# Stationary operand as neighbouring columns, stores in 128-byte pieces and another opening order in a one-core attention and MoE kernel

## The chip, the cores and the metric

The kernel runs on one core of a Trainium2 chip. The metric is the device time of one execution, in microseconds (us). The kernel before takes 589.66 us, the median of three runs (589.54 to 589.89).

## The reference, cut to what matters

```python
# attention with a decaying state, B=2, H=8, S=768, D=64
for t in range(S):
    state = gamma * state + outer(k[t], v[t])
    y[t] = scale * q[t] @ state
x = y.transpose(0, 2, 1, 3).reshape(1536, 512)
# first expert layer, 512 -> 1536 -> 512
x = x / sqrt(mean(x * x) + 1e-6) * rms_g
x = (silu(x @ w_gate) * (x @ w_val)) @ w_out
# second layer, 512 -> 2048 -> 512
h = x @ w_in
out = maximum(0.01 * h, h) @ w_out2
```

All inputs and the output are float32 (the kernel reads the weights as 64-bit numbers and makes two float32r parts of each: a high part and the rest).

## The kernel before, in words

The 1536 tokens are 12 chunks of 128 for the attention and three blocks of 512 (b = 0, 1, 2) for the two layers. The feature dimension of the weights is cut into rows or columns f of 128.

**The opening** is written out by hand, token by token, in `ORDER` (lines 42 to 56). Each engine runs the tokens that concern it in the order of this list, and none overtakes another on its engine. `load("q0")`, `load("k0")` and so on, in the order of `LOADS` (line 33), bring in what a chunk needs; a `w` in `LOADS` brings the next raw weight into one of three raw buffers (`fetch`, line 379). All these transfers are issued by SyncE into one queue. The tokens of a chunk c, with the engine in brackets: `sc` scores (TensorE), `ds` decay of the scores (VectorE), `kd` decay of k (VectorE if c is in `KD`, else eight activations on ScalarE), `qs` decay of q (GpSimd), `ou` outer product and `up` state update (TensorE, VectorE), `yi` and `he` the two parts of the chunk's output y (TensorE), `sq` square of y and `xg` y times the gain (ScalarE, both read y from PSUM), `fa` and `sa` the first two sums of the squares (VectorE). `to`, `me`, `rs`, `sp`, `xs`, `hi`, `lo` form the norm of a pair of chunks and split it into high part and rest. y has two PSUM banks, for even and odd chunks (line 226), so `yi8` may not start before `sq6` and `xg6` have read y of chunk 6.

Weights are converted in steps such as `o0:P`, `o0:1`, ... `o0:L`, for the weight o of f = 0. `:P` is two activations on ScalarE that read the raw buffer (lines 526 and 527), `:1` to `:4` are VectorE steps, `:H` the high part on ScalarE, `:L` the rest on VectorE. Step `:3` is the last that reads the raw buffer, and it calls `fetch` for the next raw weight. The raw weights come in the order g0, g1, v0, v1, o0, o1: the three `w` of `LOADS` bring the first three, `g0:3` fetches v1, and the next `:3` in the list fetches o0. The token `load` brings q11 and k11; it stands ahead of every `:3`, so v1 and o0 follow k11 in the queue.

The token `layers` marks the end of the attention on TensorE; `Mg00`, the first product of the first layer (the high parts), comes right behind it.

**The layers** run from a list of steps made by `plan`. Three kinds of product matter here, each a group of matmuls of 128x128 against 128x512:
- line 587 (`accumulate`), the down products. For the first layer (`o`) and for the blocks b > 0 of the second (`p`), the weight is the stationary operand, 128 of its columns at a time. For `p` with b = 0 the activations are stationary.
- line 706 (`seventh`), the down products of the last two groups of `p`, by sums of weights, also with the weight stationary.
- lines 554 and 858, the up products.

For `p` the 128 stationary columns are chosen by `by_quarter`: every second column of one half of 256. Two neighbouring output columns thus end up in one partition of two accumulators (m = 0 and 1). For `o` they are 128 neighbouring columns.

**The end.** When the last sums of a row of blocks are complete, `seventh` transposes the two accumulators in 32x32 blocks, with m as the innermost dimension (line 729), and stores the result in four transfers of 128 KB whose contiguous pieces are 64 floats, 256 bytes (lines 732 to 737). There are four such rows: (b, row) = (2, 0), (2, 1), (1, 0), (1, 1). Block 0 is stored last, from line 751.

Of the kernel before, what the change touches and what calls it, by code (L numbers as in the profile page):

```python
# [8 lines left out]
F32 = mybir.dt.float32  # L9
# [7 lines left out]
P = 128  # L17
# [12 lines left out]
SEVEN = 2  # L30
RAWS = 3
WARM = 7
LOADS = "q0 k0 m g s k1 q1 d q2 q3 k2 k3 q4 k4 q5 w w q6 w q7 k6 k8 k7 k5 i q8 q9 k9 q10 k10"
EARLY = 5
FIXED = 14
PLAIN = ("g0", "g1", "v0", "v1")
# [1 line left out]
BLOCKS = [512, 512, 512]  # L38


KD = (0, 1, 2, 3, 6, 7)
ORDER = """
sc0 kd0 ou0 ds0 tb ts wm1 tk he0 load kd1 up0 sc1 sq0 qs1 xg0 ou1 ds1 qs2 sc2 up1 fa0 yi1 qs3 ds2 he1 kd2 sa0 ou2 kd3
sq1 sc3 xg1 fa1 up2 qs4 yi2 ds3 kd4 ou3 sa1 sc4 up3 qs5 sc5 ds4 g0:P yi3 ds5 ou4 g1:P g0:1 he2 up4 g0:2 he3 g1:1 sq2
g0:3 to0 xg2 fa2 g1:2 sc6 me0 sa2 sq3 rs0 g0:4 sc7 xg3 ds6 v0:P yi4 kd6 ds7 ou6 qs7 kd8 he4 up6 yi5 kd7 v0:1 sq4 fa3
ou7 g0:H fa4 he5 sa3 xg4 g0:L up7 sq5 v0:2 sc8 sa4 xg5 fa5 v0:3 sc9 qs9 ds8 yi7 kd9 ds9 qs8 ou8 sp0 v0:4 to1 up8 qs10
he7 v0:H xs0 kd10 he6 me1 sa5 rs1 g1:3 sc10 v0:L sq6 g1:4 sq7 ou9 fa6 xg6 sc11 up9 fa7 xg7 sa7 yi8 ds11 g1:H yi9 hi0
qs11 ds10 ou10 o0:P he8 lo0 to2 up10 sq8 he9 sa6 me2 g1:L xg8 rs2 to3 fa8 sp1 o0:1 sq9 me3 yi10 xs1 rs3 xg9 fa9 hi1
yi11 sa8 sa9 o0:2 v1:P lo1 sp2 he10 v1:1 he11 xs2 sq10 xg10 layers Mg00 v1:2 fa10 v1:3 hi2 sa10 v1:4 Ng00 sq11 lo2
o1:P Mg10 fa11 xg11 o1:1 o0:3 Ng10 v1:H sa11 o1:2 Cg00 v1:L sp3 Cg10 o1:3 to4 xs3 Mv00 me4 o1:4 hi3 rs4 o0:4 Nv00 lo3  # L50
o0:H Mv10 g2:P o0:L Cv00 o1:H g2:1 Uo00 sp4 o1:L to5 g3:P xs4 Nv10 Mg01 me5 Lo00 hi4 rs5 Cv10 lo4 Uo10 sp5 Ng01 Lo10
xs5 Mg11 Cg01 g3:1 hi5 g2:2 g3:2 Ng11 g2:3 open lo5 Do00 Cg11 g2:4 g3:3 g2:H T0 v2:P Mg02 g3:4 T1 g3:H Ng02 v3:P g3:L
Do10 v2:1 Cg02 v3:1 Th1 v2:2 v3:2 v2:3 Tl1 Mg12 v2:4 v3:3 v2:H Ng12 g2:L v3:4 Mv01 sg2:1 Cg12 v2:L v3:H sg2:2 v3:L
sg2:H Nv01 sg2:3 sg2:L Mv11 sv2:1 Cv01 sv2:2 sg2:4 Nv11 sv2:H sv2:3 T2 sg2:h Mv02 Cv11 Th2 sg2:l Nv02 Tl2 o3:P Mv12
sv2:4 o2:P T3 Nv12 Cv02 Cv12
"""


# [1 line left out]
def chain_kernel(ctx: ExitStack, tc: tile.TileContext, qk_t, kv, w1, w2, mask, qdec, kdec, sdec, rms_g, ident, out):  # L60
    nc = tc.nc
# [8 lines left out]
    offs = [sum(BLOCKS[:b]) for b in range(NB)]  # L70
    assert sum(G1) == NF1 and sum(G2) == NF2

    units = ctx.enter_context(tc.tile_pool(name="units", bufs=UNITS))
# [30 lines left out]
    def acc_bank(i, name):  # L104
        return ps_acc.tile([P, 512], F32, tag=f"acc{i}", name=name)
# [41 lines left out]
    def decay_k(c):  # L147
        if not last(c):
            s = ch[c]
            s["kd"] = gp.tile([P, 2 * NPAIR, D], F32, tag="gh", name=f"kd{c}")  # L150
            if c in KD:
                nc.vector.tensor_tensor(
# [221 lines left out]
    def free(*keys):  # L374
        for s in slots:
            s[2].difference_update(keys)
# [181 lines left out]
    def acc_banks(name, n):  # L558
        return [acc_bank(i, f"{name}_{i}") for i in range(n)]
# [7 lines left out]
    parts = {}  # L567
    order = []

    def by_quarter(w, m):  # L570
        return w.rearrange("p (h c m) -> p h m c", h=2, m=2)[:, m // 2, m % 2]

    def accumulate(L, g, f, b, start, stop, transposed):

        if start:
            acc["b"] = acc_banks(f"a{L}_{g}_{b}", 4)
        h, l = parted.pop((L, f, b))
        w = wt[f"{L}{f}"]
        for m in range(4):
            part = slice(m * P, (m + 1) * P)  # L580
            if transposed:
                wh, wl = (w[:, i, part] if L == "o" else by_quarter(w[:, i, :], m) for i in range(2))
                terms = (wh, h), (wh, l), (wl, h)
            else:
                terms = (h[:, part], w[:, 0, :]), (h[:, part], w[:, 1, :]), (l[:, part], w[:, 0, :])
            for n, (lhs, rhs) in enumerate(terms):
                nc.tensor.matmul(out=acc["b"][m], lhsT=lhs, rhs=rhs, start=(start and n == 0), stop=(stop and n == 2))  # L587
# [3 lines left out]
    def upper(key):  # L591
        if key in made:
            x = made.pop(key)
            h = gp.tile([P, 512], F32R, tag="gh", name="g{}_{}_{}h".format(*key))
            nc.scalar.activation(out=h, in_=x, func=AF.Copy)
            halves[key] = x, h

    def lower(key):
        if key in halves:
            x, h = halves.pop(key)  # L600
            l = gp.tile([P, 512], F32R, tag="gl", name="g{}_{}_{}l".format(*key))
            nc.vector.tensor_tensor(out=l, in0=x, in1=h.bitcast(F32), op=ALU.subtract)
            parted[key] = h, l
            if key[0] == "q":
                follow(key[1], key[2])
# [9 lines left out]
    def down(gi, f, b):  # L615
        kinds, fs = groups[gi]
        L = kinds[-1]
        key = (L, f, b)
        upper(key)
        lower(key)  # L620
        accumulate(L, gi, f, b, f == fs[0], f == fs[-1], L == "o" or b > 0)
        used(f"{L}{f}")
        if f == fs[-1]:
            (evac1 if L == "o" else evac2)(gi, b, acc.pop("b"))
        placed[0] = order.index(key) + 1
# [37 lines left out]
    def gather(gi):  # L663
        for f in groups[gi][1][::2]:
            t = {(k, b): made.pop(("p", f + k, b)) for k in range(2) for b in (1, 2)}
            made["q", f, 1], made["q", f, 3], made["q", f, 2] = t[0, 1], t[1, 2], t[1, 1]
            turns[f] = t
# [22 lines left out]
    def seventh(gi, n, f):  # L690
        fs = groups[gi][1]
        key = ("q", f, n)
        if n == 1 and f == fs[0]:
            gather(gi)
        upper(key)
        lower(key)
        h, l = parted.pop(key)
        unit, half, side, start, (b, row) = SIDES[n]
        names = f"p{f}", f"p{f + 1}", f"sp{f}", f"sp{f + 1}"
        w = wt[names[unit]]  # L700
        if f == fs[0] and start:
            acc[side] = [acc_bank(i + 2 * (side == "Z"), f"{side}{gi}_{n}_{i}") for i in range(2)]
        for m in range(2):
            wh, wl = (by_quarter(w[:, i, :], 2 * half + m) for i in range(2))
            for k, (lhs, rhs) in enumerate(((wh, h), (wh, l), (wl, h))):
                nc.tensor.matmul(  # L706
                    out=acc[side][m],
                    lhsT=lhs,
                    rhs=rhs,
                    start=(start and f == fs[0] and k == 0),  # L710
                    stop=(f == fs[-2] and k == 2),
                    skip_group_check=True,
                )
        if n == 1:
            used(names[0])
        elif n == 4:
            used(names[1])
        elif n in (7, 3):
            free(names[unit])
        placed[0] = order.index(key) + 1  # L720
        if f != fs[-2]:
            return
        for m in range(2):
            dst = y2[b][:, 2 * row + m, :]
            nc.vector.tensor_tensor(out=dst, in0=acc[side][m], in1=dst, op=ALU.add)
        if gi == len(groups) - 1 and LAST[b, row] == n:
            t = units.tile([P, 16, 32, 2], F32, tag="u", name=f"turned{b}_{row}")
            for m in range(2):
                nc.vector.transpose(
                    out=t[:, :, :, m], in_=y2[b][:, 2 * row + m, :].rearrange("p (j r) -> p j r", r=32)  # L730
                )
            for i in range(4):
                o = 2 * row * P + i * 64
                nc.sync.dma_start(
                    out=out[offs[b]:offs[b] + 512, o:o + 64].rearrange("(j r) d -> r j d", r=32),
                    in_=t[32 * i:32 * i + 32].rearrange("p j c m -> p j (c m)"),
                )

    def evac2(gi, b, banks):
        first, last = gi == len(G1), gi == len(groups) - 1  # L740
# [12 lines left out]
    y2 = {}  # L753
# [70 lines left out]
    def used(key):  # L824

        n, f = key[0], int(key[1:])
        left[key] = left.get(key, 2 if doubled(n, f) else NB) - 1
        if not left[key]:
            free(key)
# [190 lines left out]
    nc.scalar.dma_start(out=kdecs[:, 0], in_=kdec)  # L1020
    load(*LOADS.split())

# [28 lines left out]
    terms = {}  # L1051
# [142 lines left out]
```

## Time and profile before

| | us |
|---|---|
| median of three runs | 589.66 |
| the profiled execution | 589.67 |
| its span, first to last instruction | 587.9 |
| TensorE matmul busy | 579.5 |
| VectorE busy | 480.8 |
| ScalarE busy | 343.5 |
| GpSimd busy | 19.5 |

All times below are counted from the start of the span. Busy time is a union of the instructions' times; a matmul's end is modelled, and it overlaps the next one, so the distance between the starts of matmuls (their pitch) says more than the duration of one. PE is the matmul stream of TensorE, PEld its weight loads, DVE VectorE, ACT ScalarE, SPq the queue of SyncE's transfers.

### The profile page before, as it was taken

To read this page: it belongs to the slowest core of one execution; us is meant where nothing else is said; L and a number is where in the kernel's file an instruction comes from. 1 tells how busy PE (TensorE), PEld (TensorE's weight loads), DVE (VectorE), ACT (ScalarE), POOL (GpSimd) and SP (SyncE) were. 2 spreads that over 40 slices of the span, in tenths; PEclk is the share of its full clock that TensorE was granted. 3 is DMA by queue.
4 is the path that set the end of the run, shared out by engine and by line. 5 is a ranking of instruction groups with operands and counts; after the bars stand their busy time and mean duration, and the time that the engine had idled before them with its cause. 6 is when DMAs were issued, how large, how long until landed. Compare 5 with 4: busy or idle time off the path is not lost.

```text
span 587.9 us, 8302 instructions
## 1 busy us (share of the span) xinstructions
PE 579.5 (99%) x3131; PEld 478.4 (81%) x3131; DVE 480.8 (82%) x865; ACT 343.5 (58%) x624; POOL 19.5 (3%) x20
## 2 busy tenths in 40 slices
PE   8899999999999999999999999999999999999997
PEld 6788788888888888888888888888888888888885
DVE  5899999999668689598589988874776679997893
ACT  2789656778655455465564766776563665574430
POOL 2332100000000000000000000000000000000000
PEclk9999999999999999999999999999999999999999
DMA  8991240524133013124130310422211110110043
GB/s 336 408 386 42 72 144 3 175 74 146 39 96 102 18 67 108 36 72 126 54 107 2 103 41 0 144 71 73 72 37 36 37 36 6 67 37 0 1 101 114
DMA packets 23319, 52.76 MB, mean 90 GB/s; under 512 B 10480, under 2 KB 10608, under 8 KB 23280
## 3 DMA queue, kind: packets, MB, share of 16 engines
q1 hardware_dynamic: 23136, 52.24, 27.0%
q8 instruction: 24, 0.39, 0.3%
q14 instruction: 15, 0.12, 0.1%
q10 hardware_dynamic: 144, 0.00, 0.0%
HBM read 49.09 MB, written 3.15 MB: 89 GB/s over the span
## 4 chain that ended last, share of the span: by engine, by line
PE 93%; DMA 5%; DVE 0%; issue 0%; SPq 0%
PE ao L587 17%; PE ap L587 15%; PE g L554 7%; PE v L554 7%; PE iX L858 7%; PE i L554 7%; PE vX L858 5%; PE gX L858 5%; PE X L706 4%; PE iZ L858 4%; DMA qkv<-in_qk_t 4%; PE Z L706 3%; PE vZ L858 2%; PE gZ L858 2%; PE iY L858 2%; PE vY L858 1%
## 5 line engine op out<-in xcount | busy, mean ns | idle before, releaser
L587 PE MATMUL ap<-w_p,gp_0h 128*128 128x512 f32 x128 | 39.4, 389 | 0.0
L554 PE MATMUL g<-xh,w_g 128*128 128x512 f32 x128 | 31.8, 390 | 0.0
L554 PE MATMUL v<-xh,w_v 128*128 128x512 f32 x128 | 31.7, 390 | 0.0
L554 PE MATMUL i<-x2h,w_i 128*128 128x512 f32 x128 | 31.6, 389 | 0.0
L587 PE MATMUL ao<-go_0h,w_o 128*128 128x512 f32 x96 | 31.5, 389 | 0.0
L587 PE MATMUL ao<-go_2h,w_o 128*128 128x512 f32 x96 | 31.5, 389 | 0.0
L587 PE MATMUL ao<-go_1h,w_o 128*128 128x512 f32 x96 | 30.5, 389 | 0.0
L554 PEld LDWEIGHTS i<-x2h,w_i 128*128 128x128 f32 x128 | 24.0, 188 | 5.1
L554 PEld LDWEIGHTS g<-xh,w_g 128*128 128x128 f32 x128 | 23.9, 188 | 5.2 <-ACT sq L258 0.2
L587 PEld LDWEIGHTS ap<-w_p,gp_0h 128*128 128x128 f32 x128 | 24.0, 188 | 5.0
L554 PEld LDWEIGHTS v<-xh,w_v 128*128 128x128 f32 x128 | 23.9, 188 | 5.0
L587 PE MATMUL ap<-w_p,gp_0l 128*128 128x512 f32 x64 | 24.9, 389 | 0.0
L587 PE MATMUL ap<-gp_2h,w_p 128*128 128x512 f32 x64 | 21.4, 394 | 0.0
L587 PEld LDWEIGHTS ao<-go_0h,w_o 128*128 128x128 f32 x96 | 18.0, 188 | 3.7
L587 PEld LDWEIGHTS ao<-go_1h,w_o 128*128 128x128 f32 x96 | 18.0, 188 | 3.7
L587 PEld LDWEIGHTS ao<-go_2h,w_o 128*128 128x128 f32 x96 | 18.0, 188 | 3.7
L587 PE MATMUL ap<-gp_1h,w_p 128*128 128x512 f32 x64 | 20.9, 394 | 0.0
L801 ACT ACTIVATE i<-i 128x512 f32<-128x512 f32 x16 | 9.5, 596 | 18.7 <-PE i L554 18.7
L858 PE MATMUL iX<-th,w_si 128*128 128x512 f32 x64 | 19.8, 390 | 0.0
L858 PE MATMUL iZ<-x2h,w_si 128*128 128x512 f32 x64 | 19.7, 389 | 0.0
L587 PE MATMUL ao<-go_0l,w_o 128*128 128x512 f32 x48 | 18.7, 389 | 0.0
L587 PE MATMUL ao<-go_1l,w_o 128*128 128x512 f32 x48 | 18.7, 389 | 0.0
(303 smaller groups left out, 1663.9 us busy)
## 6 DMA issues: line engine op xcount, KB each, us to landing
raw_i<-in_w SPq DMA_DIRECT2D x16, 512.0 KB, 3.6
raw_p<-in_w SPq DMA_DIRECT2D x16, 512.0 KB, 3.7
raw_g<-in_w SPq DMA_DIRECT2D x12, 512.0 KB, 3.6
raw_v<-in_w SPq DMA_DIRECT2D x12, 512.0 KB, 3.6
raw_o<-in_w SPq DMA_DIRECT2D x12, 512.0 KB, 4.0
qkT<-in_qk_t SPq DMA_DIRECT2D x7, 512.0 KB, 6.5
kv<-in_kv SPq DMA_DIRECT2D x7, 512.0 KB, 8.0
qkv<-in_qk_t SPq DMA_DIRECT2D x5, 512.0 KB, 11.0
```

The costliest lines, as they stand in the source:

```text
L554: nc.tensor.matmul(out=dst, lhsT=lhs, rhs=rhs, start=(n == 0), stop=(n == len(pairs) - 1), skip_group_check=True)
L587: nc.tensor.matmul(out=acc["b"][m], lhsT=lhs, rhs=rhs, start=(start and n == 0), stop=(stop and n == 2))
L706: nc.tensor.matmul(out=acc[side][m], lhsT=lhs, rhs=rhs, start=(start and f == fs[0] and k == 0), stop=(f == fs[-2] and k == 2), skip_group ...
L801: nc.scalar.activation(out=a, in_=x, func=AF.Prelu, alpha=0.01)
L858: nc.tensor.matmul(out=dst, lhsT=lhs, rhs=rhs, start=(start and n == 0), stop=(n == 5), skip_group_check=True)
```

## The change

It has three parts.
- `by_quarter` goes. In `accumulate` and in `seventh` the stationary operand is 128 neighbouring columns of `w`, for `p` as for `o`.
- The transposed result keeps m as an outer dimension, and each of the two accumulators is stored in four transfers of 64 KB with contiguous pieces of 32 floats, 128 bytes; the four follow their own transpose.
- `LOADS`, `KD` and `ORDER` are new. `KD` loses 2 and 7 and gains 9. The diff shows the parts of `ORDER` around the first chunks and from `sc7` to `layers`; the rest of the list is reordered in the same manner.

```diff
-LOADS = "q0 k0 m g s k1 q1 d q2 q3 k2 k3 q4 k4 q5 w w q6 w q7 k6 k8 k7 k5 i q8 q9 k9 q10 k10"
+LOADS = "q0 s k0 m q1 k1 d g q2 k2 k3 q3 q4 k4 q5 w w q7 q6 k6 w k7 k8 k5 q8 q9 k9 k10 i q10"
-KD = (0, 1, 2, 3, 6, 7)
+KD = (0, 1, 3, 6, 9)
 ORDER = """
-sc0 kd0 ou0 ds0 tb ts wm1 tk he0 load kd1 up0 sc1 sq0 qs1 xg0 ou1 ds1 qs2 sc2 up1 fa0 yi1 qs3 ds2 he1 kd2 sa0 ou2 kd3
...
-g0:3 to0 xg2 fa2 g1:2 sc6 me0 sa2 sq3 rs0 g0:4 sc7 xg3 ds6 v0:P yi4 kd6 ds7 ou6 qs7 kd8 he4 up6 yi5 kd7 v0:1 sq4 fa3
-ou7 g0:H fa4 he5 sa3 xg4 g0:L up7 sq5 v0:2 sc8 sa4 xg5 fa5 v0:3 sc9 qs9 ds8 yi7 kd9 ds9 qs8 ou8 sp0 v0:4 to1 up8 qs10
-he7 v0:H xs0 kd10 he6 me1 sa5 rs1 g1:3 sc10 v0:L sq6 g1:4 sq7 ou9 fa6 xg6 sc11 up9 fa7 xg7 sa7 yi8 ds11 g1:H yi9 hi0
-qs11 ds10 ou10 o0:P he8 lo0 to2 up10 sq8 he9 sa6 me2 g1:L xg8 rs2 to3 fa8 sp1 o0:1 sq9 me3 yi10 xs1 rs3 xg9 fa9 hi1
-yi11 sa8 sa9 o0:2 v1:P lo1 sp2 he10 v1:1 he11 xs2 sq10 xg10 layers Mg00 v1:2 fa10 v1:3 hi2 sa10 v1:4 Ng00 sq11 lo2
...
+sc0 wm1 ts kd0 tb tk ou0 ds0 sc1 up0 kd1 he0 load ds1 qs1 ou1 sq0 xg0 fa0 yi1 up1 qs2 sc2 kd2 sa0 he1 kd3 ds2 ou2 sq1
...
+g0:3 to0 xg3 fa3 g1:2 sc6 me0 sa3 sq2 g0:4 sc7 xg2 rs0 ds6 g0:H kd6 yi4 v0:P g0:L ou6 ds7 qs7 kd7 yi5 up6 v0:1 he4 fa2
+v0:2 kd8 sa2 ou7 v0:3 he5 up7 v0:4 sc8 sq5 g1:3 xg5 fa5 sc9 qs9 ds8 sq4 ou8 v0:H ds9 qs8 xg4 yi7 up8 kd10 fa4 sp0 kd9
+to1 sa5 he6 sa4 qs10 me1 xs0 o0:P he7 g1:4 sc10 sq7 o0:1 rs1 sq6 ou9 xg6 fa7 sc11 up9 sa7 xg7 fa6 yi8 ds11 g1:H yi9
+hi0 qs11 ds10 v1:P he8 sa6 g1:L ou10 sq8 lo0 to2 he9 xg8 up10 to3 fa8 sq9 sp1 v1:1 me2 xg9 yi10 v1:2 rs2 xs1 yi11 fa9
+hi1 sa9 he10 sa8 v1:3 me3 sp2 v1:4 sq10 to4 rs3 xs2 he11 o1:P layers Mg00 lo1 sq11 v1:H fa11 xg11 v1:L Ng00 fa10 hi2
...
 """

     def accumulate(L, g, f, b, start, stop, transposed):
...
             if transposed:
-                wh, wl = (w[:, i, part] if L == "o" else by_quarter(w[:, i, :], m) for i in range(2))
-                terms = (wh, h), (wh, l), (wl, h)
+                terms = (w[:, 0, part], h), (w[:, 0, part], l), (w[:, 1, part], h)

     def seventh(gi, n, f):
...
         for m in range(2):
-            wh, wl = (by_quarter(w[:, i, :], 2 * half + m) for i in range(2))
+            part = slice((2 * half + m) * P, (2 * half + m + 1) * P)
+            wh, wl = w[:, 0, part], w[:, 1, part]
...
-            t = units.tile([P, 16, 32, 2], F32, tag="u", name=f"turned{b}_{row}")
+            t = units.tile([P, 2, 16, 32], F32, tag="u", name=f"turned{b}_{row}")
             for m in range(2):
                 nc.vector.transpose(
-                    out=t[:, :, :, m], in_=y2[b][:, 2 * row + m, :].rearrange("p (j r) -> p j r", r=32)
+                    out=t[:, m], in_=y2[b][:, 2 * row + m, :].rearrange("p (j r) -> p j r", r=32)
                 )
-            for i in range(4):
-                o = 2 * row * P + i * 64
-                nc.sync.dma_start(
-                    out=out[offs[b]:offs[b] + 512, o:o + 64].rearrange("(j r) d -> r j d", r=32),
-                    in_=t[32 * i:32 * i + 32].rearrange("p j c m -> p j (c m)"),
-                )
+                for i in range(4):
+                    o = (2 * row + m) * P + i * 32
+                    nc.sync.dma_start(
+                        out=out[offs[b]:offs[b] + 512, o:o + 32].rearrange("(j r) d -> r j d", r=32),
+                        in_=t[32 * i:32 * i + 32, m],
+                    )
```

## Rows read from the trace of the kernel before

**Rows 1.** Busy us by stretch: PE, PEld, DVE, ACT, POOL; granted clock, DMA share, GB/s.
```profile
53.40:100.00 46.60, 46.60 (x235) 37.90 (x234) 45.55 (x76) 30.65 (x52) 2.07 (x2) 1.00 0.26 79
400.00:500.00 100.00, 100.00 (x438) 82.63 (x437) 73.05 (x131) 55.80 (x95) 0.00 (x0) 1.00 0.13 41
```
**Rows 2.** What PE waited for: line, releaser, us in total, times, longest.
```profile
PE sc L179 <- DVE a L191: 1.3, 1, 1.3
...
PE sc L179 <- DMA qkv<-in_qk_t: 1.0, 2, 0.6
...
PE y L230 <- POOL nr L298: 0.5, 1, 0.5
```
**Rows 3.** Chain that ended last, in order of time: start us, us, what.
```profile
331.28 2.72 PE ao L587 x12
...
478.13 2.80 PE ap L587 x12
...
487.82 2.80 PE Z L706 x12
```
**Rows 4.** Weight loads by shape: line, operands, count, busy us, mean ns, idle before.
```profile
L587 PEld LDWEIGHTS ao<-go_1h,w_o 128*128 128x128 f32 x96 | 18.0, 188 | 3.7
...
L587 PEld LDWEIGHTS ap<-gp_1h,w_p 128*128 128x128 f32 x64 | 12.4, 193 | 2.6
```
**Rows 5.** Timeline of TensorE's opening: start us, us, what, idle before it.
```profile
1.19 3.17 PE L185 MATMUL sc<-warm 128*128 128x512 bf16 x7 [1.19 <-DVE one_of L1016]
4.28 2.08 PE L179 MATMUL sc<-qkT 64*128 64x128 f32 x16
6.39 0.73 PE L205 MATMUL u<-kv,kd 128*64 128x64 f32 x16
...
42.12 1.16 PE L179 MATMUL sc<-qkT 64*128 64x128 f32 x16
43.21 2.07 PE L230 MATMUL y<-qs,state 64*64 64x128 f32 x32
...
53.42 2.12 PE L554 MATMUL g<-xh,w_g 128*128 128x512 f32 x8
```
**Rows 6.** Timeline of ScalarE around the first conversion of o.
```profile
39.13 2.01 ACT L160 ACTIVATE kd<-kv,kdecs 128x64 f32<-128x64 f32 x8
41.04 1.05 ACT L258 ACTIVATE sq<-y 128x512 f32<-128x512 f32 x2
41.99 2.15 ACT L266 ACTIVATE xg<-y,g_sb 128x128 f32<-128x128 f32 x8
...
45.45 0.74 ACT L526 ACTIVATE wa_o<-raw_o 128x512 f32<-128x512 f32 x1
46.04 0.73 ACT L527 ACTIVATE wb_o<-raw_o 128x512 int32<-128x512 uint32 x1
...
48.79 1.18 ACT L266 ACTIVATE xg<-y,g_sb 128x128 f32<-128x128 f32 x4
```
**Rows 7.** SyncE's issues of raw o, then the first one: KB, us to landing.
```profile
35.64 5.56 SPq L384 DMA_DIRECT2D raw_o<-in_w  x2
...
raw_o<-in_w SPq DMA_DIRECT2D x1, 512.0 KB, 8.5
```
**Rows 8.** Single microseconds while raw o was under way, columns as in Rows 1.
```profile
39.00:40.00 1.00, 1.00 (x24) 1.00 (x22) 1.00 (x3) 1.00 (x5) 0.64 (x1) 1.00 1.01 410
...
42.00:43.00 1.00, 1.00 (x22) 0.93 (x18) 1.00 (x4) 1.00 (x6) 0.00 (x0) 1.00 0.77 274
```
**Rows 9.** The last stretches, columns as in Rows 1: stores and clock.
```profile
564.00:565.00 1.00, 1.00 (x6) 0.85 (x5) 1.00 (x3) 0.00 (x0) 0.00 (x0) 1.00 1.02 214
...
584.00:584.25 0.25, 0.18 (x1) 0.00 (x0) 0.25 (x2) 0.00 (x0) 0.00 (x0) 1.00 1.02 369
...
586.75:587.00 0.25, 0.00 (x0) 0.00 (x0) 0.00 (x0) 0.00 (x0) 0.00 (x0) 0.58 0.00 0
```
**Rows 10.** SyncE's issues of the stores: start us, us to the last one's end.
```profile
561.88 13.28 SPq L734 DMA_DIRECT2D out<-turned  x16
582.90 2.37 SPq L751 DMA_DIRECT2D out<-y2acc  x4
```

More of the change, by code (lines that the diff above doesn't have):

```diff
@@ L38 @@
 BLOCKS = [512, 512, 512]
-KD = (0, 1, 2, 3, 6, 7)
+KD = (0, 1, 3, 6, 9)
 ORDER = """
-sc0 kd0 ou0 ds0 tb ts wm1 tk he0 load kd1 up0 sc1 sq0 qs1 xg0 ou1 ds1 qs2 sc2 up1 fa0 yi1 qs3 ds2 he1 kd2 sa0 ou2 kd3
-sq1 sc3 xg1 fa1 up2 qs4 yi2 ds3 kd4 ou3 sa1 sc4 up3 qs5 sc5 ds4 g0:P yi3 ds5 ou4 g1:P g0:1 he2 up4 g0:2 he3 g1:1 sq2
-g0:3 to0 xg2 fa2 g1:2 sc6 me0 sa2 sq3 rs0 g0:4 sc7 xg3 ds6 v0:P yi4 kd6 ds7 ou6 qs7 kd8 he4 up6 yi5 kd7 v0:1 sq4 fa3
-ou7 g0:H fa4 he5 sa3 xg4 g0:L up7 sq5 v0:2 sc8 sa4 xg5 fa5 v0:3 sc9 qs9 ds8 yi7 kd9 ds9 qs8 ou8 sp0 v0:4 to1 up8 qs10
@@ L47 @@
-he7 v0:H xs0 kd10 he6 me1 sa5 rs1 g1:3 sc10 v0:L sq6 g1:4 sq7 ou9 fa6 xg6 sc11 up9 fa7 xg7 sa7 yi8 ds11 g1:H yi9 hi0
-qs11 ds10 ou10 o0:P he8 lo0 to2 up10 sq8 he9 sa6 me2 g1:L xg8 rs2 to3 fa8 sp1 o0:1 sq9 me3 yi10 xs1 rs3 xg9 fa9 hi1
-yi11 sa8 sa9 o0:2 v1:P lo1 sp2 he10 v1:1 he11 xs2 sq10 xg10 layers Mg00 v1:2 fa10 v1:3 hi2 sa10 v1:4 Ng00 sq11 lo2
-o1:P Mg10 fa11 xg11 o1:1 o0:3 Ng10 v1:H sa11 o1:2 Cg00 v1:L sp3 Cg10 o1:3 to4 xs3 Mv00 me4 o1:4 hi3 rs4 o0:4 Nv00 lo3
-o0:H Mv10 g2:P o0:L Cv00 o1:H g2:1 Uo00 sp4 o1:L to5 g3:P xs4 Nv10 Mg01 me5 Lo00 hi4 rs5 Cv10 lo4 Uo10 sp5 Ng01 Lo10
@@ L52 @@
[L52 to L55, printed above, removed]
+sc0 wm1 ts kd0 tb tk ou0 ds0 sc1 up0 kd1 he0 load ds1 qs1 ou1 sq0 xg0 fa0 yi1 up1 qs2 sc2 kd2 sa0 he1 kd3 ds2 ou2 sq1
@@ new lines @@
+qs3 sc3 xg1 up2 sc4 qs4 ds3 ou3 fa1 kd4 yi2 up3 ds4 sc5 qs5 g0:P yi3 ds5 ou4 g1:P sa1 g0:1 he3 up4 g0:2 he2 g1:1 sq3
+g0:3 to0 xg3 fa3 g1:2 sc6 me0 sa3 sq2 g0:4 sc7 xg2 rs0 ds6 g0:H kd6 yi4 v0:P g0:L ou6 ds7 qs7 kd7 yi5 up6 v0:1 he4 fa2
+v0:2 kd8 sa2 ou7 v0:3 he5 up7 v0:4 sc8 sq5 g1:3 xg5 fa5 sc9 qs9 ds8 sq4 ou8 v0:H ds9 qs8 xg4 yi7 up8 kd10 fa4 sp0 kd9
+to1 sa5 he6 sa4 qs10 me1 xs0 o0:P he7 g1:4 sc10 sq7 o0:1 rs1 sq6 ou9 xg6 fa7 sc11 up9 sa7 xg7 fa6 yi8 ds11 g1:H yi9
+hi0 qs11 ds10 v1:P he8 sa6 g1:L ou10 sq8 lo0 to2 he9 xg8 up10 to3 fa8 sq9 sp1 v1:1 me2 xg9 yi10 v1:2 rs2 xs1 yi11 fa9
@@ new lines @@
+hi1 sa9 he10 sa8 v1:3 me3 sp2 v1:4 sq10 to4 rs3 xs2 he11 o1:P layers Mg00 lo1 sq11 v1:H fa11 xg11 v1:L Ng00 fa10 hi2
+me4 o0:2 Mg10 sa10 v0:L Cg00 xg10 lo2 Ng10 o0:3 o1:1 sp3 sa11 Cg10 o1:2 Mv00 rs4 xs3 o1:3 hi3 Nv00 o0:4 lo3 o0:H Mv10
+g2:P o0:L Cv00 to5 g2:1 Uo00 sp4 o1:4 Nv10 me5 Lo00 o1:H Mg01 g3:P xs4 rs5 o1:L hi4 Cv10 sp5 lo4 Ng01 Uo10 Mg11 xs5
+Cg01 Lo10 hi5 Ng11 g2:2 g3:1 open g2:3 Do00 Cg11 lo5 g2:4 T0 g2:H Mg02 v2:P g3:2 T1 Ng02 g3:3 Th1 v2:1 Do10 g3:4 Cg02
+Tl1 g3:H v3:P g3:L v2:2 Mg12 v3:1 v2:3 v3:2 v2:4 Ng12 v3:3 v2:H Mv01 g2:L Cg12 v3:4 sg2:1 v3:H v2:L Nv01 v3:L Mv11
@@ L56 @@
+sg2:2 sv2:1 sg2:H sv2:2 sg2:3 sv2:H sg2:L Nv11 Cv01 Mv02 sv2:L Cv11 sv2:3 sg2:4 Nv02 sv2:4 sg2:h T2 sv2:h Mv12 sg2:l
+Th2 T3 Nv12 Cv12 Cv02
 """
@@ L568, in chain_kernel @@
     order = []
-    def by_quarter(w, m):
-        return w.rearrange("p (h c m) -> p h m c", h=2, m=2)[:, m // 2, m % 2]
     def accumulate(L, g, f, b, start, stop, transposed):
```

## The prediction

> **What bounds the kernel now.** The busy time by stretch comes first [rows 1]: from 53.4 us on TensorE is busy without a gap, while VectorE is busy 73 us of 100 in a late stretch. The list of what TensorE waited for [rows 2] says the same from the other side: the largest entries are 1.3, 1.0 and 0.5 us, all in the opening. So behind the opening a change is worth what it takes from the pitch of the matmuls, and in the opening what it does to the waits. Two more views are read for that: the chain in order of time, whose pieces without a gap give the pitch [rows 3], and the timelines of TensorE, ScalarE and SyncE around one conversion step [rows 5 to 7].
>
> **Stationary columns.** Twelve matmuls with 128 neighbouring columns as stationary operand (`ao`) take 2.72 us, a pitch of 226.7 ns; twelve with every second column (`ap` for b > 0, `Z`) take 2.80 us, 233.3 ns [rows 3]. The weight loads differ by as much, 188 against 193 ns [rows 4]. `ao` and `ap` run the same line with the same shapes and only the stride differs, so I take the whole difference for the stride. It concerns 2 groups x 4 f x 2 blocks x 12 matmuls = 192 on line 587 and 2 groups x 7 products x 2 pairs x 6 matmuls = 168 on line 706, 360 in all or 30 twelves: 30 x 0.08 = 2.40 us less. TensorE is the bound there and VectorE has a quarter of its time free [rows 1], so it all reaches the end.
>
> A rule speaks against this. The Trainium skill, "Advanced Engine Details and Errata", section "SBUF Cachelines", says that reads of the SBUF run at full speed as long as two of them fall into each 16-byte line. Every second float32 is just that, so by the rule the stride would cost nothing and this term would be 0 instead of 2.40. The rows above show a cost; I go by them.
>
> **Stores.** 16 transfers of 128 KB become 32 of 64 KB, each again 512 pieces. SyncE's 16 issues took 13.3 us from 561.9 on with waits for data in between [rows 10]; 32 at no more than half a microsecond would end by about 578. The DMA engines moved 214 GB/s at a full share [rows 9], so a 256-byte piece costs an engine 256 x 16 / 214 = 19 ns. A piece of half the size costs at least half of that (9.5 ns) and, as the nearest row has it, at most the same; which of the two doesn't matter. At 19 ns the four rows of blocks, each 4,096 pieces or 256 per engine, take 4 x 4.9 = 19.6 us from about 562 and are through by 582, and the last stores are first issued at 582.9 [rows 10]. Cover: about 1 us. Cost 0. The transposes write as many elements as before on an engine that nothing waits for there.
>
> **The opening.** I follow ScalarE's order, since one step in it has moved across others. Before, `o0:P` stands behind `xg7`, `g1:H` and `hi0`, and ran at 45.45 [rows 6]. Raw o0 was issued at 35.64 and took 8.5 us to land: 44.14 [rows 7]. It took so long because the queue was full: 410 GB/s at a full share at 39 us, still 274 at 42 [rows 8]. In the new list `o0:P` stands behind `kd10` and ahead of `sq7`, `sq6`, `xg6`, `xg7`. Nothing in the change brings o0 earlier: its issue still follows q11, k11 and v1 in the one queue, ahead of it are the same 24 chunks, tables and four raw weights, and the rate is the same. So I let it land at 44.14 again.
>
> `kd10` was done at 41.1 before [rows 6] and will not be later, since k10 stands one place further forward; ScalarE then has nothing to do until 44.14, and everything behind `o0:P` waits in its queue. From there: `o0:P` 1.32 us (45.45 to 46.77), two squares and the gains of one chunk 2.0 us (41.04 to 43.06, half of the eight gains counted) [rows 6], so `xg6` ends at 44.14 + 1.32 + 2.02 = 47.5. `yi8` needs the bank that `xg6` frees; it started at 43.21 before, without a wait, behind the scores of chunk 11 [rows 5]. That is 4.3 us later. The work that TensorE has ahead of `yi8` is the same set of tokens, and would be done by about 43 again, so it idles some 4.3 us. VectorE is held in the same hole: `o0:1` needs `o0:P`, and stands ahead of `fa7`, `up9` and `ds11`.
>
> From `yi8` to the first product of the layer it was 53.42 - 43.21 = 10.2 us [rows 5], with the wait of 0.5 in it [rows 2]. It names GpSimd, but `yi11` needs the bank that `xg9` frees, and those gains ended at 49.97 [rows 6], when the wait did. In the new list `v1:P` stands ahead of `sq8`, `xg8`, `sq9`, `xg9` on ScalarE where `o0:P` stood before, so this wait stays, and the stretch stays at 10.2. `to4` moves ahead of it: 0.2 us later here, given back behind. VectorE is 98% busy from 53.4 to 100 us [rows 1], but it loses the hole together with TensorE and keeps its lead, so I add nothing.
>
> The waits that the new order may remove (the 1.0 for q7 and q8 [rows 2]) are ahead of `yi8`, which is then paced by the landing of o0 alone; they are worth nothing in this case. The same holds for `KD`: it moves the decay of two chunks from VectorE to ScalarE and one back, net 2.0 us more on ScalarE [rows 6], all ahead of the hole.
>
> **The clock** is the unknown price. After TensorE's last matmul, about 584.2, its granted clock left the upper level (2.4 GHz) for the lower (1.2 GHz) at about 586.8, after 2.6 us without work [rows 9]. An idle stretch of 4.3 us may do the same. At the start, the 16 matmuls of the first scores took 2.08 us against 1.16 later, while the outer products at 6.39 already ran at full speed; that is 5.2 us after the first matmul at 1.19 [rows 5]. So the price lies between 0 (no fall) and 5.2 x 0.5 = 2.6 us (half speed as long as at the start, nothing of it hidden). I exclude a gain: no row shows TensorE faster. No row shows a stop of this length with work behind it, and part of the slow stretch would lie under ScalarE's gains; I take 1.2 and keep both ends.
>
> **Sum**, against the profiled execution (589.67, of which 1.8 lie outside the span; the median is 589.66): 589.67 - 2.40 + 4.28 + 1.2 = 592.75, rounded 592.7. Own range of this case 590.8 (shorter hole by 0.7, no fall) to 594.2 (full price of the clock).
>
> **Rivals.**
> - *Landing earlier, about the same time.* 16 engines share each transfer, and at 42 us they are 77% busy [rows 8], so some are through before the slowest. Were they even, o0 would land near 42.2 instead of 44.14. The hole shrinks by 1.9, short enough (2.4 us) to leave the clock alone: 589.67 - 2.40 + 2.34 = 589.6. Against it: the mix of transfers is unchanged.
> - *The other side: no hole, faster.* The mechanism is the landing of o0 against the end of `kd10`. If o0 is there by 39.8 us, `xg6` ends by 43.1 and `yi8` doesn't wait; then the opening saves the 0.5 at `yi11` and about 0.2 at the scores of chunk 8, whose chunk now has the 64 KB table i behind it instead of ahead: 589.67 - 2.40 - 0.7 = 586.6. For it: everything else in the new order fits the landings of before (q7 ahead of q6, kd2 on an idle ScalarE). Against it: o0 would have to land 4.3 us earlier out of a full queue.
> - *The change doesn't do what it says:* a load of every second column is no slower of itself, and the 0.08 per twelve have another cause, in the tiles or the neighbours of `p`. The 2.40 stay, and with the hole the time is 592.7 + 2.4 = 595.1. Against it: line 587 has both pitches with the same shapes [rows 3].
>   The rule on 16-byte lines from the Trainium skill ("Advanced Engine Details and Errata", "SBUF Cachelines") would give this time.
> - *Stores pile up.* If a 128-byte piece cost over 20 ns, the last stores would queue behind the others. At twice the 19 ns the four rows take 39 us, to 601, and the end is some 15 us later, near 608.
>   The Trainium skill, "DMA: Bandwidth & Descriptors", section "Specifications", asks for at least 512 bytes per piece and says that smaller ones are read, modified and written; the 256-byte pieces of before already fall under that and ran at 214 GB/s [rows 9].
>
> **How the numbers follow.** Chances: forecast 0.57, landing earlier 0.12, no hole 0.25, stride free 0.03, stores 0.03. The bound between same and changed is 0.2%, 1.2 us, about what a measurement of this kernel can tell from no change. Faster: 0.25. Same: 0.12. Slower: 0.57 + 0.03 + 0.03 = 0.63. The case without a hole is too likely to leave out, so the range goes from its time, 586.4, to the upper end of the forecast, 594.2.
>
> **What would show it.** Stationary term: twelves of `ap` (b > 0), `X`, `Z` at 2.72 instead of 2.80. Hole: ScalarE idle ahead of the first `wa_o<-raw_o` (L526 there), released by DMA, three to five us, and TensorE idle as long ahead of a line 230 group near 43 us; `Mg00` at about 58 instead of 53.4. Clock: a granted clock of 0.5 somewhere from 45 to 53 us. Stores: landing of `out<-turned` not much above 2.5 us and the last stores landing as before. The forecast is wrong if raw o lands by 40 us or if `yi8` doesn't wait for `xg6`.

## Result and profile after

The changed kernel takes 594.14 us, the median of five runs (594.07 to 595.19), against 589.66 (by now also the median of five). The ratio is 1.0081, with a 95% interval of 1.0068 to 1.0094. The change made the kernel slower by 4.5 us. Three of the five runs lie at 594.1, the other two at 595.0 and 595.2. The profiled execution takes 594.14 us, its span is 592.4.

Where the time went is seen in the same views as before. In the changed kernel line 583 is `accumulate` (587 before), line 703 `seventh` (706), line 855 the half products (858). First everything that TensorE waited for: line, releaser, us in total, times, longest.

```profile
PE y L230 <- issue: 4.0, 1, 4.0
PE sc L185 <- DVE one_of L1013: 1.2, 1, 1.2
PE sc L179 <- DMA qkT<-in_qk_t: 1.1, 1, 1.1
PE sc L179 <- DMA qkv<-in_qk_t: 0.9, 1, 0.9
```

One wait of 4.0 us is new; in [rows 2] the longest is 1.3. "Issue" means that the view shows no releaser for it. The timeline of TensorE has it ahead of `yi8`, as [rows 5] had `yi8` at 43.21 without a wait and `Mg00` at 53.42:

```profile
43.31 1.16 PE L179 MATMUL sc<-qkT 64*128 64x128 f32 x16
48.52 3.30 PE L230 MATMUL y<-qs,state 64*64 64x128 f32 x32 [4.05 <-issue]
...
60.14 2.12 PE L554 MATMUL g<-xh,w_g 128*128 128x512 f32 x8
```

ScalarE's timeline shows what lies behind it ([rows 6] before):

```profile
38.75 2.03 ACT L160 ACTIVATE kd<-kv,kdecs 128x64 f32<-128x64 f32 x8 [0.96 <-DMA kv<-in_kv]
45.20 0.66 ACT L526 ACTIVATE wa_o<-raw_o 128x512 f32<-128x512 f32 x1 [4.42 <-DMA raw_o<-in_w]
45.76 0.66 ACT L527 ACTIVATE wb_o<-raw_o 128x512 int32<-128x512 uint32 x1
46.32 1.08 ACT L258 ACTIVATE sq<-y 128x512 f32<-128x512 f32 x2
47.27 2.19 ACT L266 ACTIVATE xg<-y,g_sb 128x128 f32<-128x128 f32 x8
```

ScalarE stands for 4.42 us ahead of `o0:P` until raw o0 has landed, with the squares and gains of chunks 6 and 7 queued behind. `yi8` starts when half of the eight gains, those of chunk 6, are through. VectorE stands in the same hole, `o0:1` being ahead of `fa7`:

```profile
45.89 0.43 DVE L456 TENSOR_SCALAR wa_o<-wa_o 128x512 f32<-128x512 f32 x1 [3.77 <-ACT wa_o L526]
```

SyncE issued raw o0 at 36.15, half a microsecond later than before, and it took 9.0 us instead of 8.5 [rows 7]:

```profile
36.15 1.60 SPq L384 DMA_DIRECT2D raw_o<-in_w  x2
...
raw_o<-in_w SPq DMA_DIRECT2D x1, 512.0 KB, 9.0
```

Then the busy time by stretches; the last three columns are granted clock, DMA share and GB/s. First the kernel before, whose clock is 1.00 from 40 to 60 us:

```profile
40.00:50.00 10.00, 9.59 (x178) 8.37 (x174) 9.96 (x21) 9.95 (x30) 3.90 (x4) 1.00 0.39 145
50.00:60.00 10.00, 9.93 (x97) 8.35 (x98) 9.95 (x21) 9.05 (x19) 0.00 (x0) 1.00 0.24 64
```

In the changed kernel the clock falls at the end of the hole, from 2.4 to 1.2 GHz, and is back at 52 us (most lines are single microseconds):

```profile
10.00:12.00 2.00, 1.91 (x18) 1.69 (x20) 1.32 (x3) 0.00 (x0) 0.00 (x0) 0.59 1.06 413
...
44.00:45.00 1.00, 0.47 (x10) 0.28 (x6) 0.00 (x0) 0.00 (x0) 0.00 (x0) 1.00 0.39 160
47.00:48.00 1.00, 0.00 (x0) 0.00 (x0) 1.00 (x4) 1.00 (x4) 0.00 (x0) 0.94 0.00 0
48.00:49.00 1.00, 0.47 (x5) 0.51 (x7) 1.00 (x2) 1.00 (x5) 0.00 (x0) 0.50 0.00 0
50.00:51.00 1.00, 1.00 (x14) 1.00 (x12) 1.00 (x3) 1.00 (x2) 0.37 (x1) 0.50 0.00 0
51.00:52.00 1.00, 1.00 (x16) 0.83 (x14) 1.00 (x2) 1.00 (x2) 1.00 (x1) 0.85 0.00 0
52.00:53.00 1.00, 1.00 (x28) 1.00 (x26) 1.00 (x1) 0.15 (x2) 0.43 (x1) 1.00 0.00 0
```

The first line belongs to another low stretch, from about 10.3 to 13.8 us. The profile of `old_loads` below has one there too, those of the other kernels have none. It costs this kernel nothing that the rows show: what it may delay, the matmuls up to the scores of chunk 11 (at 43.31, against 42.2 to 43.2 in the other profiles with the new order), lies ahead of a `yi8` that waits for o0, and the loads ran at 400 GB/s and more in every stretch of 8 us from 8 to 40.

Last, pieces of the chain in order of time, to be held against [rows 3], and the weight loads, against [rows 4]:

```profile
478.14 2.72 PE ap L583 x12
...
493.10 2.72 PE Z L703 x12
495.82 2.79 PE X L703 x12
```
```profile
L583 PEld LDWEIGHTS ap<-gp_1h,w_p 128*128 128x128 f32 x64 | 12.0, 188 | 2.5
```

The twelves of `ap` and `Z` are at 2.72 and the loads at 188 ns: the first part of the change does what it says. Of the seven twelves of `X` and `Z` in each half, the chain has three of `X` at 2.79 and, in the other half, one at 2.83. The view of line 703 shows what its engine waited for ahead of them (us in total, times):

```profile
DVE gq_6l L598: 0.4, 2
```

Two more lines of that view have 0.2 us, once each, for `gq_7l` and `gq_4l`. From the two profiled executions the balance is: `yi8` 48.52 - 43.21 = 5.31 us later; from `yi8` to `Mg00` 11.62 instead of 10.21, 1.41 more; from `Mg00` to the end of the span 532.3 instead of 534.5, 2.2 less. Together 4.5.

### The profile page after: what moved, and what is told of

It reads as the page before. It is cut to its first block, busy times and chain, and to the rows that moved or that the text cites. A ratio compares the mean times of both kernels' runs of the same rounds, so it can differ in the third digit from the quotient of the medians.

```text
span 592.4 us, 8333 instructions
## 1 busy us (share of the span) xinstructions
PE 580.1 (98%) x3131; PEld 479.2 (81%) x3131; DVE 480.1 (81%) x864; ACT 346.3 (58%) x632; POOL 19.6 (3%) x20
## 4 chain that ended last, share of the span: by engine, by line
PE 92%; DMA 6%; issue 1%; DVE 0%; POOL 0%; SPq 0%
PE ao L583 17%; PE ap L583 14%; PE g L554 7%; PE v L554 7%; PE iX L855 7%; PE i L554 7%; PE vX L855 5%; PE gX L855 5%; PE X L703 4%; PE iZ L855 4%; PE Z L703 3%; PE vZ L855 2%; PE gZ L855 2%; DMA qkv<-in_qk_t 2%; PE iY L855 2%; DMA raw_g<-in_w 2%
## 5 line engine op out<-in xcount | busy, mean ns | idle before, releaser
L583 PE MATMUL ao<-go_2l,w_o 128*128 128x512 f32 x48 | 18.7, 389 | 0.0
## 6 DMA issues: line engine op xcount, KB each, us to landing
qkv<-in_qk_t SPq DMA_DIRECT2D x5, 512.0 KB, 10.3
```

## Experiments

All ratios are to the kernel before, run on the same chip.

**The parts apart.** `products_stores` keeps the new products and stores and takes the opening of before; `opening` is the reverse.

```diff
-LOADS = "q0 s k0 m q1 k1 d g q2 k2 k3 q3 q4 k4 q5 w w q7 q6 k6 w k7 k8 k5 q8 q9 k9 k10 i q10"
+LOADS = "q0 k0 m g s k1 q1 d q2 q3 k2 k3 q4 k4 q5 w w q6 w q7 k6 k8 k7 k5 i q8 q9 k9 q10 k10"
-KD = (0, 1, 3, 6, 9)
+KD = (0, 1, 2, 3, 6, 7)
...
```

> The changed products and stores with LOADS, KD and ORDER of before. Theory (the stride costs 6.7 ns a matmul, 360 of them; the stores cost nothing): 589.66 - 2.40 = 587.3 us, twelves of ap, X and Z at 2.72, Mg00 at 53.4 as before. Rival (products or stores cost time at the end): above 589. Rival (the changed kernel lost time outside the opening too): the last stores land later than 2.1 us after their issue.

Measured: 587.54 us, ratio 0.9965 (0.9952 to 0.9978), 2.1 us faster than before and 6.6 faster than the changed kernel. Stores as expected: each of the 32 lands in a median of 1.9 us, the last four in 2.1 as before.

> The kernel before with the new LOADS, KD and ORDER alone. Theory (all of the loss is in the opening): 594.14 + 2.40 = 596.5 us, Mg00 at 60.1, ScalarE idle 4.4 us ahead of the first wa_o. Rival (products and opening do not add): outside 595.9 to 597.2.

Measured: 596.61 us, ratio 1.0118 (1.0103 to 1.0133). The two parts add: -2.1 and +6.9 make +4.8, against 4.5 measured for both. All of the loss is in the opening. That the median meets the expected 596.5 is luck, though: two runs took 595.8 and 596.0 us, the other two 597.2 and 597.6, and the median lies between the pairs. With the shorter pair the parts make -2.1 + 6.2 = +4.1, against 4.4 for the three shorter runs of the changed kernel. In the profiled execution, one of the long ones, ScalarE idles 5.16 us and `Mg00` comes at 61.25, not 4.4 and 60.1 as expected; its busy time by microseconds, with the columns as above, shows the clock:

```profile
47.00:48.00 1.00, 0.00 (x0) 0.00 (x0) 1.00 (x5) 1.00 (x6) 0.00 (x0) 0.63 0.00 0
...
53.00:54.00 1.00, 1.00 (x18) 1.00 (x16) 0.15 (x1) 0.21 (x1) 0.00 (x0) 0.50 0.00 0
54.00:55.00 1.00, 1.00 (x30) 1.00 (x28) 0.53 (x2) 1.00 (x4) 0.00 (x0) 0.96 0.00 0
```

Here the low level lasts from about 47.3 to 54 us, in the changed kernel's profile from about 47.9 to 51.3.

**Stores apart.** `products_256` is `products_stores` with the transposes and stores of before:

```diff
-            t = units.tile([P, 2, 16, 32], F32, tag="u", name=f"turned{b}_{row}")
+            t = units.tile([P, 16, 32, 2], F32, tag="u", name=f"turned{b}_{row}")
...
```

> Products with neighbouring columns, opening and stores of before: the transposes interleave the two accumulators and the stores go in 256-byte pieces, so that the columns of blocks 1 and 2 land in other places of the output. Theory (stores cost nothing either way): the same as products_stores within 0.2 us, 587.3. Rival (128-byte pieces cost time at the end): faster than products_stores by over 0.3 us.

Measured: 587.50 us against 587.54. Pieces of 128 or 256 bytes make no difference to the time of this kernel.

**The step out of place.** `o0_late` moves two tokens of the changed kernel:

```diff
-to1 sa5 he6 sa4 qs10 me1 xs0 o0:P he7 g1:4 sc10 sq7 o0:1 rs1 sq6 ...
+to1 sa5 he6 sa4 qs10 me1 xs0 he7 g1:4 sc10 sq7 rs1 sq6 ...
-hi1 sa9 he10 sa8 v1:3 me3 sp2 v1:4 sq10 to4 rs3 xs2 he11 o1:P layers ...
+hi1 sa9 he10 sa8 v1:3 me3 sp2 v1:4 sq10 to4 rs3 xs2 he11 o0:P o1:P layers ...
-me4 o0:2 Mg10 ...
+me4 o0:1 o0:2 Mg10 ...
```

> The changed kernel with o0:P moved behind he11 and o0:1 ahead of o0:2, all else as changed. Theory (ScalarE's wait for raw o0 ahead of sq7, sq6, xg6 is the hole): yi8 follows the scores of chunk 11 at 44.4 without a wait, Mg00 about 54.6, no fall of the clock: 594.14 - 5.5 = 588.6 us. Rival (the rest of the new order keeps TensorE waiting): Mg00 later than 57, over 591 us.

Measured: 588.16 us, ratio 0.9975 (0.9965 to 0.9985). `yi8` has no wait, and no clock falls:

```profile
42.46 1.16 PE L179 MATMUL sc<-qkT 64*128 64x128 f32 x16
43.55 1.96 PE L230 MATMUL y<-qs,state 64*64 64x128 f32 x32
...
53.93 2.12 PE L554 MATMUL g<-xh,w_g 128*128 128x512 f32 x8
```

Two tokens, out of 317 in `ORDER`, carry 6.0 of the 6.6 us that lie between the changed kernel and `products_stores`, the fall of the clock included.

**The clock.** `fill` puts matmuls that compute nothing into the hole:

```diff
+    def filler():
+        for _ in range(30):
+            nc.tensor.matmul(out=nrm["bank"][:, 272:512], lhsT=warm[:, :P], rhs=warm[:, :240], start=True, stop=True)
...
-... xg7 fa6 yi8 ds11 ...
+... xg7 fa6 fill yi8 ds11 ...
```

> The changed kernel with 30 more warm matmuls (128x128 against 128x240, into unused columns of the norm bank) on TensorE ahead of yi8. They lie in the hole, some 3 of its 4 us. Theory (the clock fall behind the hole costs 1.0 to 1.4 us): no granted clock under 1.0 between 45 and 55 us, 592.9 us. Rival (the slow stretch is hidden under ScalarE's gains): 594.1. Rival (the fill delays yi8): above 594.5.

Measured: 592.35 us, ratio 1.0045 (1.0030 to 1.0060); the clock stays up, and 1.5 us of the hole are left:

```profile
47.00:48.00 1.00, 0.00 (x0) 0.00 (x0) 1.00 (x5) 1.00 (x6) 0.00 (x0) 1.00 0.00 0
48.00:49.00 1.00, 0.76 (x14) 0.79 (x16) 1.00 (x2) 1.00 (x6) 0.00 (x0) 1.00 0.00 0
```

The medians differ by 594.14 - 592.35 = 1.8 us, more than the 1.0 to 1.4 that I expected. Not all of it is the clock: `o0:P` ran at 44.90 in the profile of `fill` instead of 45.20, and `yi8` started at 48.24 instead of 48.52. What the clock takes is seen behind that: `yi8` to `Mg00` takes 10.4 us in `fill`, 11.6 in the changed kernel and 13.1 in `opening` with its longer fall, so 1.2 or 2.7 us, by the time that the low level lasts. That fits the two pairs of runs of `opening`, whose mean clock is 0.997 in the short ones and 0.994 in the long ones. It would fit the runs of the changed kernel too, three at 594.1 and two about 1 us longer, but there only one execution was profiled, and the mean clock can't tell the lengths apart because of the other low stretch at 10 us.

**Where o0 loses its time.** `other_queue` loads raw o0 through ScalarE's queue:

```diff
-            nc.sync.dma_start(out=raw[key].rearrange("p n two -> p (n two)"), in_=src.bitcast(I32))
+            queue_of = nc.scalar if key == "o0" else nc.sync
+            queue_of.dma_start(out=raw[key].rearrange("p n two -> p (n two)"), in_=src.bitcast(I32))
```

> The changed kernel with raw o0 loaded through ScalarE's queue instead of SyncE's; its place in the order of instructions stays. Theory (o0 is late because it stands at the end of SyncE's full queue): it lands 3 to 4 us after its issue, near 40, o0:P waits less than 1.5 us, yi8 less than 1 us, 588.6 to 589.5 us. Rival (the DMA engines are the limit and a second queue does not help): landing after 43, 593 us or more.

Measured: 592.01 us, ratio 1.0038 (1.0023 to 1.0053). My expectation failed:

```profile
35.43 0.34 ACTq L385 DMA_DIRECT2D raw_o<-in_w  x1
...
43.64 0.67 ACT L527 ACTIVATE wa_o<-raw_o 128x512 f32<-128x512 f32 x1 [2.26 <-DMA raw_o<-in_w]
```

It landed 8.2 us after its issue, not 3 to 4, at 43.6 us as the rival had it, and 1.6 us earlier than in the changed kernel. `yi8` waited 2.7 us, and the clock did not fall in the profile, whose execution took 591.22 us. Two of the four runs took 592.6 and 592.7 us at a mean clock of 0.996 and 0.997, against 0.999 in the two short ones, so in those two it may well have fallen. The queues' shares of the 16 engines, first in 37 to 39 us, then in 39 to 41, show how o0 was served (q10 is ScalarE's queue):

```profile
q1 hardware_dynamic: 242, 0.80, 102.6%
q10 hardware_dynamic: 4, 0.02, 2.0%
...
q10 hardware_dynamic: 99, 0.41, 50.5%
q1 hardware_dynamic: 107, 0.40, 49.7%
```

Up to 38.5 us the engines served SyncE's queue alone, although o0 had been issued at 35.4; from 39 us on the two had equal shares. So a second queue passed little of what already stood in the first. Why it wasn't served sooner isn't shown; it had carried a small table before, so this was not its first use.

**The loads.** `old_loads` is the changed kernel with `LOADS` of before; `fill_old_loads` and `o0_late_old_loads` are the kernels above with it.

```diff
-LOADS = "q0 s k0 m q1 k1 d g q2 k2 k3 q3 q4 k4 q5 w w q7 q6 k6 w k7 k8 k5 q8 q9 k9 k10 i q10"
+LOADS = "q0 k0 m g s k1 q1 d q2 q3 k2 k3 q4 k4 q5 w w q6 w q7 k6 k8 k7 k5 i q8 q9 k9 q10 k10"
```

> The changed kernel with LOADS of before. In the changed kernel the DMA engines moved 274 and 259 GB/s between 2 and 6 us against 352 and 316 before, and raw o0 landed at 45.1 instead of 44.1. Theory (the new LOADS shifts the whole stream by 1 us, and the hole ends with the landing of o0): o0:P at 44.2, 593.1 us, give or take 1 us if the clock falls at another moment. Rival (the later landing comes from the order, which frees raw buffers later): 594.1.

Measured: 594.27 us, ratio 1.0076 (1.0061 to 1.0091): no gain. Yet its profile has `o0:P` at 44.27, 0.9 earlier than the changed kernel's. With a fall of the clock behind it whose length may vary from run to run, half a microsecond can't be seen in a median of four runs (593.55 to 594.42); inconclusive.

> The kernel fill (30 warm matmuls in the hole) with LOADS of before. No clock falls in either, so the two differ by the loads alone. Theory (the new LOADS make raw o0 land 0.6 to 0.9 us later, as 44.27 against 44.84 to 45.20 in the profiles): 592.35 - 0.75 = 591.6 us. Rival (executions scatter by as much, and LOADS do not matter): 592.2 to 592.5.

Measured: 591.85 us (591.67 to 592.00) against 592.35 for `fill` (592.30 to 592.57). Without the clock the loads show: the new `LOADS` cost 0.5 us, a little less than expected.

All profiles together say the same of the landing of raw o0 (its issue plus its time to landing). In eight with the old `LOADS` it lies at 44.0 to 44.3 us, whether `ORDER` is old or new and whether o0 was issued at 33.9 or at 35.9. In four with the new `LOADS` (all but `other_queue`) it lies at 44.4, 44.8, 44.9 and, in the changed kernel, 45.15. The two groups differ as well in what the engines moved in the first 8 us, 269 to 274 GB/s against 237 to 262; first the kernel before, then the changed one:

```profile
0.00:8.00 8.00, 6.26 (x43) 3.62 (x44) 2.47 (x10) 1.49 (x2) 0.20 (x4) 1.00 0.77 269
...
0.00:8.00 8.00, 6.78 (x31) 3.66 (x31) 1.39 (x10) 1.49 (x2) 0.20 (x4) 1.00 0.74 237
```

So with the old `LOADS` the order of steps doesn't set the landing, and the new `LOADS` move it. Which of its places does it isn't shown, nor why the four profiles differ by 0.8.

> The changed kernel with o0:P behind he11, o0:1 ahead of o0:2 and LOADS of before. Theory (hole and later stream are the whole loss): 588.6 - 1.0 = 587.6 us, up to 0.5 less if the wait at yi11 goes. Rival (the new order needs the new LOADS): waits of TensorE for chunks, 588.6 or more.

Measured: 587.96 us, ratio 0.9971 (0.9960 to 0.9982); 0.2 less than `o0_late`, whose nine runs spread from 587.76 to 588.74, so that this 0.2 is not clear of noise. The gain of up to 0.5 at `yi11` is partly there (its wait is 0.2 instead of 0.5), but a new wait of 0.34 for the mean of a pair stands ahead of `sp2`. Compared with `products_stores` (587.54), the new order is 0.4 slower than the old even when the hole is closed.

**The wait at `yi11`.** `o0_behind_hi1` takes `products_stores` and moves the conversion of o0 back by a few more steps:

```diff
-qs11 ds10 ou10 o0:P he8 ... sp1 o0:1 sq9 ...
+qs11 ds10 ou10 he8 ... sp1 sq9 ...
-yi11 sa8 sa9 o0:2 v1:P lo1 sp2 ...
+yi11 sa8 sa9 o0:P v1:P lo1 o0:1 o0:2 sp2 ...
```

> The kernel products_stores with o0:P moved behind hi1 on ScalarE, and o0:1, o0:2 behind lo1 on VectorE. Theory (the wait of 0.5 us at yi11, which the profile puts down to GpSimd, is for xg9, which stood behind o0:P): the wait goes, xg9 ends 1.3 us earlier, 587.54 - 0.48 = 587.1 us. Rival (the wait is for GpSimd): it stays, 587.5. Rival (v1 and o0 come too late for the first products): a wait ahead of the products of v or o, 587.6 or more.

Measured: 588.35 us, ratio 0.9977 (0.9968 to 0.9986), 0.8 slower than `products_stores`. My expectation failed; the wait stays:

```profile
50.00 1.09 PE L230 MATMUL y<-qs,state 64*64 64x128 f32 x16 [0.47 <-POOL nr L298]
```

```profile
46.76 0.60 ACT L258 ACTIVATE sq<-y 128x512 f32<-128x512 f32 x1 [1.22 <-PE y L246]
...
48.72 1.18 ACT L266 ACTIVATE xg<-y,g_sb 128x128 f32<-128x128 f32 x4
```

ScalarE now idles 1.22 us ahead of `sq8`, because the heads of chunk 8 are not done before 46.7; `xg9` ends at 49.90, against 49.97 before, and `yi11` starts at 50.00. GpSimd's step `nr` had ended at 49.46, half a microsecond earlier. So the wait ends with `xg9`, not with GpSimd; but `o0:P` had stood in time that ScalarE had to spare. Moved, it makes another wait, 0.8 us, at a `sp` token further on.

**How far a stride matters.** `stride4` is the kernel before with every fourth column:

```diff
-        return w.rearrange("p (h c m) -> p h m c", h=2, m=2)[:, m // 2, m % 2]
+        return w.rearrange("p (c m) -> p m c", m=4)[:, m]
```

> The kernel before with every fourth column as the stationary operand of p instead of every second one; the columns of blocks 1 and 2 land in the wrong places. Theory (what counts is how many columns share 16 bytes: 4, 2 and now 1): loads clearly over 193 ns, twelves of ap, X, Z over 2.9 us, over 592 us in all. Rival (any step but one costs the same): 193 ns and 2.80, 589.7.

Measured: 590.81 us, one run. The loads went up, the pitch hardly:

```profile
L587 PEld LDWEIGHTS ap<-gp_1h,w_p 128*128 128x128 f32 x64 | 17.8, 310 | 0.2
```
```profile
478.43 2.82 PE ap L587 x12
```

A load takes 310 ns instead of 193, but twelve matmuls take 2.82 us instead of 2.80. Both readings that I had put against each other are wrong: the step counts, but beside running matmuls nearly all of it is hidden. It shows where a load has to wait for its data first: the four twelves of `X` that wait for low parts take 2.94 to 2.95 us instead of 2.82. Of the 1.1 us that the kernel lost, these four make about half, the other 26 twelves the rest.

## Why the prediction was right or wrong

The direction and the mechanism were right, place by place: the hole stands ahead of the first `wa_o<-raw_o`, TensorE idles ahead of `yi8` from 44.5 to 48.5 us, VectorE stands with it, and the clock falls behind it. The size was not. I said 592.7 and at most 594.2; measured are 594.14 in the median and, by the ratio of the runs, in which the two longer ones weigh in, 589.66 x 1.0081 = 594.4, on the upper edge of the range and past it.

The step that failed is the landing of o0, and with it the term of the hole. I let o0 land "at 44.14 again" because nothing in the change would bring it earlier and "the rate is the same". The rate was not the same: the new `LOADS` moved less in the first 8 us, and o0 landed at 45.15. The hole put `yi8` 5.31 us later instead of 4.28. That is 1.03 of the 1.4 us by which the profiled execution misses the forecast; the stationary columns and the stretch behind `yi8` make 0.2 each. Term by term:

- **Stationary columns, -2.40:** -2.1 (`products_stores`) to -2.2 (`products_256`, and the stretch behind `Mg00` in the profiles). The stride is what the pitch of these twelves cost. By the rule of the Trainium skill that the prediction draws on ("Advanced Engine Details and Errata", section "SBUF Cachelines") this term would be nothing; the measured 2.1 to 2.2 us decide against it here. The 0.2 to 0.3 that are missing lie in the four twelves of `X` that stay at 2.79 to 2.83. Their weight loads wait for the low parts that VectorE makes (`gq_6l`, `gq_7l`, `gq_4l`), as they did before. The claim that all of the term reaches the end was too broad: a few of the twelves were not bound by the pitch.
- **Stores, 0:** right; `products_256` differs by 0.04 us.
- **The landing of o0, "44.14 again":** 44.4 to 45.2 in four profiles with the new `LOADS`, 44.0 to 44.3 in eight with the old. I looked only for what might bring o0 earlier, not for what might set it back. `fill` against `fill_old_loads` puts 0.5 us on `LOADS`. The other half microsecond of the changed kernel is a difference between executions with the same `LOADS`; its cause stays open.
- **The hole, 4.28 later at `yi8`:** 5.31, the above included. The three steps from landing to `yi8` took 3.4 us, as summed (3.3).
- **From `yi8` to `Mg00`, unchanged but for the clock:** 10.4 us in `fill`, where the clock stays up, against 10.2 forecast and 0.2 for `to4`. Right.
- **The clock, 1.2 between 0 and 2.6:** 1.2 in the profiled execution, 2.7 in the long fall of `opening`. That 1.2 was hit is luck: I had taken it as about the middle between two ends, not from a row. I took the time from the first matmul to full speed at the start, 5.2 us, as the longest that the low level lasts; in `opening` it lasted 6.6 us, and its price lies just past my upper end. It is the two longer runs of the changed kernel that carry the ratio past the range; whether they had the long fall isn't shown. That a stop of 2.4 us would leave the clock alone, as the first rival has it, rested on the one row at the end of the kernel; the fall at 10.3 us, behind stops of at most 1.1 us, shows that a row of that kind doesn't make a limit.
- **The rivals:** the landing didn't come early. Closing the hole, as in the rival on the other side, gave 588.16 where I had 586.6; with the old `LOADS` 587.96. Its 0.7 from the opening was not there: the wait at `yi11` went down by 0.3 only where another came, and the order without the hole is 0.4 slower than the old one.

Two small slips changed nothing: the lower end of the range, 586.4, lies 0.2 under the 586.6 of the rival that it goes by, and the weight loads differ by 5 ns where the pitch differs by 6.6.

Of the 6.6 us that the new opening costs, the experiments account for 6.0 by the two tokens and perhaps 0.2 by `LOADS` where the hole is closed; what is left, 0.4, is the rest of the order, and I did not take it apart. The best of the kernels that leave the output in its place is `products_stores` at 587.54 us, faster than both: the products and stores of the change with the opening of before.

## What to carry to other kernels

A hand-written order is read engine by engine: for each instruction that waits for a transfer, find what stands behind it on its engine and work out when the transfer lands from the bytes ahead of it in its queue, not from the usual time to landing (a median of 3.6 to 4.2 us for the raw weights of a whole run, 8.4 to 10.1 for raw o0 here). A step that was harmless in a gap holds up everything when it is moved past work that others wait for. Where a change opens an idle stretch on TensorE of the 4 to 5 us seen here, count the clock behind it as part of the price, and give it more than one size (1.2 and 2.7 us here). And where the order of the loads changes, the landings are to be worked out anew.

## What was not expected of the hardware

- The granted clock fell in the three profiles with an idle stretch of 4.0 to 4.8 us on TensorE and stayed at 1.00 over 2.7 us in that of `other_queue`, though two of that kernel's runs, about 1.3 us longer at a lower mean clock, may have lost it. Once down, it stayed so until about 51 us in one execution and 54 in another, with matmuls running all the while. The length of one stop doesn't tell everything: in the changed kernel's profile the clock also fell at 10.3 us, where the longest stop between matmuls had been 1.1 us, and `fill`, with a stop of 1.4 us in the same place, kept 1.00.
- A transfer issued on a second queue, empty at the time, was not served for 3 us while the first queue was full, then at an equal share.
- A weight load of every fourth float32 column takes 310 ns against 188 for neighbours, yet the pitch rises only from 226.7 to 235 ns; with every second column it is 193 and 233. The pitch doesn't follow the duration of the load.
